# Moving four pieces of VectorE work in the first steps of a fused attention and two-layer kernel

## The chip, the cores and the metric

The kernel runs on one core of a Trainium2 chip. Times are device microseconds of one execution. TensorE (PE in the rows) multiplies matrices, VectorE (DVE), ScalarE (ACT) and GpSimd (POOL) work on elements, SyncE (SP) issues the DMAs. Each engine runs its own instructions in the order in which the program writes them and waits for other engines by semaphores.

## The reference

```python
# q, k, v: 4 batches, 8 heads, 576 positions, 64 wide
scores = scale * q @ k.T
ret = scores * Dmat              # gamma ** (i - j) where i >= j, else 0
x = (ret @ v), heads side by side   # 2304 tokens x 512
h = x @ w_in                     # 512 -> 2048, weights arrive as float64
g = h * sigmoid(1.702 * h)
x = g @ w_out                    # 2048 -> 512
h = x @ w2_in                    # 512 -> 1024
solu = h * softmax(h)
ln = (solu - mean) / sqrt(var + 1e-6) * g_ln
out = ln @ w2_out                # 1024 -> 512
```

## The kernel before

**Stages.** First comes the attention, in eight pairs of (batch, head pair) units, `k` from 0 to 7. Then the first layer runs in 24 steps. A step `s` is a generation `g` (a quarter of the 2048 hidden features), a pair `p` of token tiles (2 x 384 tokens) and a half `i` of the generation's features. Steps 0 to 5 are generation 0: steps 0 and 1 are the first pair of token tiles, 2 and 3 the second, 4 and 5 the third. The second layer follows at the end.

**A step's products.** `emit_h` does not multiply a 2 x 2 block of tiles with eight products but with seven, by sums of x and of the weights (Strassen's scheme in a form with few additions). It uses four PSUM banks, A, C, B and D. TensorE (line 705) makes, in this order, A, C, B, then A and C again on top, then D, then B again on top. VectorE adds the intermediate results (line 711): c12 from B before B gets its second product, then C, then c21, D and B. ScalarE then applies the gate (lines 682 and 684), and the low part of the result is a subtraction (line 685), on VectorE in steps 1 and 3 and mostly on GpSimd elsewhere. `emit_y` (line 779) multiplies the gated features with `w_out`. In steps 1 and 3 it ends with the second token tile, whose four results go to the banks that the step's own h leaves.

**Two parts of each number.** Matrices are held as a high and a low part, so that each product is three products of TensorE. ScalarE writes the high part by a cast (line 660 for x, line 292 for weights), GpSimd the low part by a subtraction (lines 662 and 293).

**Work beside the products.** Three kinds of VectorE work are put between the steps:

- *Conversions* (`convert`, lines 277 to 279): float64 weights, loaded by DMA into one of two raw buffers, become float32 in three instructions, by way of a PSUM bank named `conv`. Once one is done, the next load into the same buffer is issued (line 263).
- *Combinations* (`queue_combine`, line 284, 128x256): four differences of converted weights, t1 to t4, of which t2 and t4 need the ones before. ScalarE's casts of the weights (line 292) follow.
- *Sums of x* (`combine_x`, lines 653 and 284, 128x768): s1, s2, s3 and s4 of the next pair of token tiles, from which x's parts are split.

Conversions and combinations stand in one queue, `bg`. `slot(n)` takes work of cost n from its front at the place in the program where it is called: a conversion costs 3, a combination 0.5. The table `PACE` gives n for the first steps, one number inside `emit_h` after the last additions and one at the step's end. Casts of weights that a combination feeds are held for a later `slot`, three at a time.

Of the kernel before, what the change touches and what calls it, by code (L numbers as in the profile page):

```python
# [39 lines left out]
PAIRS = [[p if g % 2 == 0 else NPR - 1 - p for p in range(NPR)] for g in range(GENS)]  # L40
# [108 lines left out]

WARM = 7  # L150
LATE = 3
PACE = ((2, 6), (0, 6), (5, 0), (0, 6), (6, 0), (5, 0))


class Build:
# [195 lines left out]
    def pace(self, s, part):  # L351


        if s < len(PACE):
            return PACE[s][part]
        most = lambda t, b: ((6, 0), (6, 0), (6, 0), (6, 0), (6, 3), (6, 3))[t % 6][b]
# [651 lines left out]
    def run(self):  # L1008
# [8 lines left out]
        def spin(n):  # L1017
            for _ in range(n):
                nc.tensor.matmul(wb[:, 0:P], warm, warm, start=True, stop=True)
# [4 lines left out]
        def load_w():  # L1024
            dst, piece = self.first_loads.pop(0)
            self.load_raw(dst, self.source(piece))
# [13 lines left out]
        sums, split_x = self.combine_x(0)  # L1040

        def make_x(*js):
            for j in js:
                split_x(j)
                self.xready += 1
# [3 lines left out]
        for k in range(NPAIR):  # L1049
            u = 2 * k  # L1050
            nxt = k + 1 < NPAIR
            if k + 2 < NPAIR:
                self.decay_q(u + 4, u + 5)
            if k == 0:
                pt, o = self.bank("T0"), []
                self.scores(0)
                spin(2)
                self.scale_v(0)
                self.states(0, pt)
                o.append(self.bank("o0"))  # L1060
                self.within(0, o[0], True)
                self.scores(1)
                ends = [self.bank("e0")]
                self.last_scores(0, ends[0])
                self.last_masks(0, ends[0])
                spin(4)
                self.scale_v(1)
                self.states(1, pt)
                self.scan(0, pt)
                o.append(self.bank("o1"))  # L1070
                self.within(1, o[1], True)
                pt = self.bank("T1")
                self.scale_v(2)
                self.states(2, pt)
                ends.append(self.ybank("e1"))
                self.across(0, o, ends, False)
                self.scale_v(3)
                self.states(3, pt)
                for i in range(2):
                    self.take(i, o[i], False)  # L1080
                for i in range(2):
                    self.take(i, ends[i], True)
                self.scan(1, pt)
                self.scores(2)
                self.last_scores(1, ends[0])
                self.last_masks(1, ends[0])
                self.scores(3)
            else:
                if nxt:
                    self.scale_v(u + 2)  # L1090
                if k > 1:
                    self.scores(u)
                    self.scores(u + 1)
                o, ends = [self.bank(f"o{u}")], [self.bank(f"e{k}")]
                o.append(self.bank(f"o{u + 1}"))
                for i in ((), (), (), (), (0,), (1,), (3,), (2,))[k]:
                    sums[i]()
                self.slot((0, 0, 0, 0, 0.5, 0.5, 0, 6)[k])
                ends.append(self.ybank(f"e{u + 1}"))
                self.across(k, o, ends, True)  # L1100
                if nxt:
                    pt = self.bank(f"T{k + 1}")
                    self.states(u + 2, pt)
                for i in range(2):
                    self.take(u + i, ends[i], True)
                if not nxt:
                    steps = self.emit_h(0)
                    next(steps)
                for i in range(2):
                    self.within(u + i, o[i], False)  # L1110
                if nxt:
                    self.scale_v(u + 3)
                    self.states(u + 3, pt)
                    self.last_scores(k + 1, ends[0])
                    make_x(*((), (), (), (), (1,), (2,), (4,))[k])
                    self.slot((0, 3, 3, 1, 0, 0, 0)[k])
                    self.scan(k + 1, pt)
                    self.last_masks(k + 1, ends[0])
                for i in range(2):
                    self.take(u + i, o[i], False)  # L1120
            if k == 0:
                for i, part in ((NU, 0), (NU, 1), (NU + 1, 1)):
                    self.load_unit(i, part)
                load_w()
                self.load_unit(NU + 1, 0)
            for i in (u + NU, u + 1 + NU):
                if k and i < 2 * NPAIR:
                    for part in range(2):
                        self.load_unit(i, part)
            for _ in range((0, 0, 0, 0, 1, 1, 2, 2)[k]):  # L1130
                load_w()
            make_x(*((), (0,), (3,), (5,), (), (), (), (6,))[k])
# [3 lines left out]
        for g, p, i in STEPS:  # L1136
            s = 6 * g + 2 * PAIRS[g].index(p) + i
            at = PAIRS[g].index(p)
            if s == 0:
                self.queue_rest()  # L1140
            self.last = g == GENS - 1
            after = PAIRS[g][at + 1] if at + 1 < NPR else None
            self.quiet = 0 < g < GENS - 1 and i == 0 and after is not None
            for j in self.emit_h(s) if s else chain([0], steps):
                while s == 0 and self.first_loads:
                    load_w()
                if s == 0:
                    self.store_x(p, j)
                if s + 1 == NSTEP and j == 1:
                    self.flush()  # L1150
                if s == 1 and j == 1:
                    self.slot(0)
                if s == 1 and j == 2:
                    sums[3]()
                if s == 2 and j == 4:
                    sums, split = self.combine_x(PAIRS[0][2])
                    for fn in sums:
                        fn()
                if i and after is not None:
                    if g == 0:  # L1160
                        if s != 1 or j != 6:
                            split(j)
                            self.store_x(after, j)
                    else:
                        self.load_x(after, j)
            if s == 1:
                sums[2]()
                split(6)
                self.store_x(after, 6)
            if s == 0:  # L1170
                sums, split = self.combine_x(PAIRS[0][1])
                for fn in sums[:2]:
                    fn()
            if s + 1 == NSTEP:
                self.open_second()
                for k, u in ((2, (1, 1)), (3, (2, 0)), (4, (2, 1))):
                    self.fetch(u, self.wo[k].rearrange("r (a b) -> r a b", a=2))
                self.nys = 0
                ys, y1, y2 = (self.split_y(p) for p in range(3))
                for fn in ys:  # L1180
                    fn()
            f = list(range(FG * g, FG * g + FG))
            y = lambda t, a, n, *r, **k: self.emit_y(g, p, t, f[a:a + n], *r, **k)
            if s == 0:
                y(0, 0, 2, True, False)
                y(1, 0, 2, bank=self.bank)
            elif s == 1:
                y(0, 2, 2, False)
                y(1, 2, 2, add=True, bank=self.bank)
            elif g == 0 and not i:  # L1190
                y(0, 0, 2, True, False)
            elif g == 0:
                y(0, 2, 2, False)
                if after is not None:
                    y(1, 0, FG, bank=self.bank)
            elif i:
                y(0, 0, FG)
            else:
                pg, pp, _ = STEPS[s - 1]
                self.emit_y(pg, pp, 1, range(FG * pg, FG * pg + FG))  # L1200
            self.done.add(("y", s))
            self.ring = self.bank if g == 0 and i == 0 else self.ybank
            self.quiet = g > 0 and i == 0 and at + 1 < NPR
            if s not in (2, 4):
                self.slot(self.pace(s, 1))
            self.quiet, self.ring = False, self.bank
        for fn in y1[:6] + y2[:4]:
            fn()
# [126 lines left out]
```

## Time and profile before

| | |
|---|---|
| median of 3 runs | 648.93 us (648.71 to 649.03) |
| profiled execution | 648.17 us, of which the span of the trace is 646.4 us |
| TensorE, VectorE, ScalarE, GpSimd busy | 638.0 (99%), 448.9 (69%), 283.9 (44%), 304.5 (47%) us |
| HBM, mean over the span | 187 GB/s |

The busy shares are means over the whole span. The stage that the change touches lies between about 34 and 125 us, and a row there says more than the share. In a row of the timeline the first number is the start in us from the span's start and the second the time from the start of the first to the end of the last of the instructions that the row holds. What stands in brackets at the end is the time in which the engine was idle ahead of it, and what ended that.

### The profile page before, as it was taken

The page shows a single profiled execution, that of the slowest core. Times are in us where ns is not written, and L with a number is a line of the kernel's source. Part 1 is how long each engine was busy: PE and PEld are TensorE (multiplying, and loading weights), DVE is VectorE, ACT ScalarE, POOL GpSimd, SP SyncE. Part 2 cuts the span into 40 slices and gives each one's busy share as a digit, 9 for nine tenths or more (in the row PEclk, how much of TensorE's full clock was granted, in tenths as well). Part 3 has the DMA queues.
Part 4 walks back from the last instruction along what each step waited for, and adds up shares of the span by engine and source line. Part 5 has one row for each costly group of instructions (what it writes and reads, how often), then busy time and mean ns, then how long its engine had stood idle before and what let it go on. Part 6 is the DMA issues. An engine that isn't in the chain of part 4 may idle for free.

```text
span 646.4 us, 11295 instructions
## 1 busy us (share of the span) xinstructions
PE 638.0 (99%) x4316; PEld 597.9 (93%) x4316; DVE 448.9 (69%) x746; ACT 283.9 (44%) x614; POOL 304.5 (47%) x312
## 2 busy tenths in 40 slices
PE   8999999999999999999999999999999999999998
PEld 7989989999999999999999999998888888888887
DVE  2998979746477587567576454455998977787770
ACT  3566564746434343334343424343444552454231
POOL 3498595955335574336574424352324430442100
PEclk9999999999999999999999999999999999999999
DMA  8999466662575835756644959489100000000001
GB/s 330 411 416 419 179 230 242 239 234 97 188 318 203 334 131 163 275 229 256 260 149 137 361 219 337 165 301 359 48 18 32 34 17 16 34 17 16 33 32 50
DMA packets 30006, 121.78 MB, mean 188 GB/s; under 512 B 3328, under 2 KB 3840, under 8 KB 29952
## 3 DMA queue, kind: packets, MB, share of 16 engines
q1 hardware_dynamic: 29808, 120.99, 49.5%
q8 instruction: 34, 0.56, 0.3%
q14 instruction: 20, 0.16, 0.1%
q10 hardware_dynamic: 144, 0.07, 0.0%
HBM read 88.28 MB, written 32.77 MB: 187 GB/s over the span
## 4 chain that ended last, share of the span: by engine, by line
PE 83%; DVE 2%; issue 0%; ACT 0%; DVEq 0%
PE y L779 28%; PE o L933 15%; PE h L843 13%; PE h_B L705 7%; PE h_A L705 7%; PE h_C L705 7%; PE h_D L705 3%; PE zT L907 2%; DVE mem L284 1%; DVE mem L711 0%; DVE mem L653 0%; DVE conv L278 0%; DVE mem L279 0%; DVE conv L277 0%; DVE g L685 0%
## 5 line engine op out<-in xcount | busy, mean ns | idle before, releaser
L685 POOL TENSOR_TENSOR g<-mem,g 128x384 fp32r<-128x384 f32 x84 | 87.7, 1055 | 143.1 <-ACT mem L684 140.0
L293 POOL TENSOR_TENSOR win<-mem,win 128x256 fp32r<-128x256 f32 (+2 forms) x59 | 53.8, 941 | 56.7 <-ACT win L292 52.6
L779 PE MATMUL y<-g,wo 128*128 128x384 f32 x432 | 77.9, 334 | 0.0
L779 PEld LDWEIGHTS y<-g,wo 128*128 128x128 f32 x432 | 75.0, 188 | 0.3 <-DVE mem L788 0.2
L711 DVE TENSOR_TENSOR mem<-h_B,mem 128x384 f32<-128x384 f32 x48 | 26.6, 555 | 65.1 <-PE h_B L705 65.0
L788 DVE TENSOR_TENSOR mem<-y,mem 128x384 f32<-128x384 f32 x76 | 38.2, 550 | 26.6 <-PE y L779 26.4
L284 DVE TENSOR_TENSOR mem<-mem 128x256 f32<-128x256 f32 (+2 forms) x49 | 47.8, 1005 | 0.7
L662 POOL TENSOR_TENSOR x<-mem,x 128x384 fp32r<-128x384 f32 x42 | 43.4, 1065 | 5.6 <-ACT x L660 5.6
L843 PE MATMUL h<-ut,win 128*128 128x512 f32 x168 | 42.9, 390 | 0.0
L894 POOL TENSOR_TENSOR mem<-mem 128x1 f32<-128x1 f32 x18 | 10.3, 573 | 68.7 <-DVE mem L893 62.5
L293 POOL TENSOR_TENSOR ws<-mem,ws 128x512 fp32r<-128x512 f32 (+1 forms) x32 | 36.5, 1159 | 10.9 <-ACT ws L292 10.8
L933 PE MATMUL o<-u,zs 128*128 128x512 f32 (+1 forms) x171 | 41.7, 388 | 0.0
L719 ACT COPY mem<-h_A 128x384 f32<-128x384 f32 x24 | 11.6, 485 | 67.9 <-PE h_A L705 66.9
L779 PE MATMUL y<-g,wo0dt.float32r 128*128 128x384 f32 x216 | 40.8, 335 | 0.1
L779 PE MATMUL y<-g,wo1dt.float32r 128*128 128x384 f32 x216 | 40.3, 334 | 0.0
L849 DVE TENSOR_TENSOR mem<-h,mem 128x512 f32<-128x512 f32 x36 | 24.6, 687 | 22.4 <-PE h L843 12.5
L933 PE MATMUL o<-wo,zs 128*128 128x512 f32 (+1 forms) x171 | 40.0, 378 | 0.0
L779 PEld LDWEIGHTS y<-g,wo0dt.float32r 128*128 128x128 f32 x216 | 37.6, 188 | 0.6 <-DVE mem L279 0.4
L779 PEld LDWEIGHTS y<-g,wo1dt.float32r 128*128 128x128 f32 x216 | 37.7, 188 | 0.0
L843 PEld LDWEIGHTS h<-ut,win 128*128 128x128 f32 x168 | 31.4, 188 | 6.4
L933 PEld LDWEIGHTS o<-wo,zs 128*128 128x128 f32 x171 | 31.0, 188 | 6.0
L933 PEld LDWEIGHTS o<-u,zs 128*128 128x128 f32 x171 | 29.9, 189 | 5.1
(154 smaller groups left out, 1506.1 us busy)
## 6 DMA issues: line engine op xcount, KB each, us to landing
x<-xd SPq DMA_DIRECT2D x42, 768.0 KB, 8.6
xd<-x SPq DMA_DIRECT2D x21, 768.0 KB, 4.7
mem<-in_w SPq DMA_DIRECT2D x28, 512.0 KB, 5.5
in<-in_att SPq DMA_DIRECT2D x16, 576.0 KB, 9.9
in<-in_att SPq DMA_DIRECT2D x16, 544.0 KB, 9.2
out<-mem SPq DMA_DIRECT2D x17, 256.0 KB, 2.0
mem<-in_w2in SPq DMA_DIRECT2D x8, 512.0 KB, 4.0
wdt<-ws SPq DMA_DIRECT2D x8, 512.0 KB, 5.4
```

Of the source, the lines that this page charges most:

```text
L284: self.nc.vector.tensor_tensor(o, a, b, ALU.subtract)
L293: self.nc.gpsimd.tensor_tensor(lo, src, f32(hi), ALU.subtract)
L662: (engine or self.nc.gpsimd).tensor_tensor(x[:, 1, k], a[:, k], f32(x[:, 0, k]), ALU.subtract)
L685: engine.tensor_tensor(gs[:, 1], u, f32(gs[:, 0]), ALU.subtract)
L705: nc.tensor.matmul(o, w[:, c:c + P], x[j][:, m, k], start=(start and i == 0), stop=(stop and i == 5), skip_group_check=True,)
L711: add = lambda o, a, b: nc.vector.tensor_tensor(o, a, b, ALU.add)
L779: nc.tensor.matmul(o[m], w[:, c:c + P], gs[:, b], start=(begin and i == 0), stop=(end and i == 2),)
L788: nc.vector.tensor_tensor(y[:, m], o[m], y[:, m], ALU.add)
L843: nc.tensor.matmul(o, a[:, l, k], w[:, m], start=(start and i == 0), stop=(stop and i == 5), skip_group_check=True,)
L849: add = lambda o, a, b: nc.vector.tensor_tensor(o, a, b, ALU.add)
L907: nc.tensor.transpose(pt[:, b * P:(b + 1) * P], u[:, w:w + P], ident)
L933: nc.tensor.matmul(o[:, 0:n], z[:, a, k], w[:, b, p * n:(p + 1) * n], start=(k == 0 and i == 0), stop=(k == FB - 1 and i == 2),)
```

## The change

It moves four pieces of work to other places in the program. No instruction is added or removed on an engine that computes.

- One combination goes from the fifth pair of the attention (`k` = 4) to the end of the fourth (`k` = 3).
- The last two conversions of step 0 go ahead of the first two sums of x for the second pair.
- The four sums of x for the third pair go from the middle of step 2's h to its end. The four combinations of step 2 stay behind them.
- One conversion goes from the end of step 2's h into step 3's h, after D's product.

```diff
-PACE = ((2, 6), (0, 6), (5, 0), (0, 6), (6, 0), (5, 0))
+PACE = ((2, 6), (0, 6), (0, 0), (0, 6), (6, 0), (5, 0))
...
-                self.slot((0, 0, 0, 0, 0.5, 0.5, 0, 6)[k])
+                self.slot((0, 0, 0, 0, 0, 0.5, 0, 6)[k])
...
-                    self.slot((0, 3, 3, 1, 0, 0, 0)[k])
+                    self.slot((0, 3, 3, 1.5, 0, 0, 0)[k])
...
-                if s == 2 and j == 4:
-                    sums, split = self.combine_x(PAIRS[0][2])
-                    for fn in sums:
-                        fn()
+                if s == 3 and j == 5:
+                    self.slot(3)
...
-            if s == 0:
-                sums, split = self.combine_x(PAIRS[0][1])
-                for fn in sums[:2]:
+            if s == 2:
+                sums, split = self.combine_x(PAIRS[0][2])
+                for fn in sums:
                     fn()
+                self.slot(2)
...
             if s not in (2, 4):
                 self.slot(self.pace(s, 1))
+            if s == 0:
+                sums, split = self.combine_x(PAIRS[0][1])
+                for fn in sums[:2]:
+                    fn()
```

On VectorE, between step 0's combinations and step 1's c12 (the two 768-wide rows are the sums of x):

```order
 L284 TENSOR_TENSOR mem<-mem 128x256 x4
+L277 TENSOR_SCALAR conv<-mem 128x512
+L278 SCALAR_TENSOR_TENSOR conv<-mem,conv 128x512
+L279 SCALAR_TENSOR_TENSOR mem<-mem,conv 128x512
+L277 TENSOR_SCALAR conv<-mem 128x512
+L278 SCALAR_TENSOR_TENSOR conv<-mem,conv 128x512
+L279 SCALAR_TENSOR_TENSOR mem<-mem,conv 128x512
 L653 TENSOR_TENSOR mem<-mem 128x768
 L284 TENSOR_TENSOR mem<-mem 128x768
```

The same two conversions stood right behind these two sums before, so conversions and sums have changed places.

On VectorE in step 2, from c12 on (the three rows that move are c21, D and B; the 768-wide ones are the third pair's sums):

```order
 L711 TENSOR_TENSOR mem<-h_B,mem 128x384
 L711 TENSOR_TENSOR h_C<-h_C,mem 128x384
+L711 TENSOR_TENSOR mem<-h_B,mem 128x384
+L711 TENSOR_TENSOR h_D<-h_D,mem 128x384
+L711 TENSOR_TENSOR h_B<-mem 128x384
 L653 TENSOR_TENSOR mem<-mem 128x768
 L284 TENSOR_TENSOR mem<-mem 128x768
 L284 TENSOR_TENSOR mem<-mem 128x2x384
 L284 TENSOR_TENSOR mem<-mem 128x768
-L711 TENSOR_TENSOR mem<-h_B,mem 128x384
-L711 TENSOR_TENSOR h_D<-h_D,mem 128x384
-L711 TENSOR_TENSOR h_B<-mem 128x384
```

The additions c21, D and B now stand ahead of the four sums.

On VectorE behind that, from step 2's combinations into step 3's h (g_1101 and g_1102 are the first two gates of step 3; the first line 711 row is its c12):

```order
 L284 TENSOR_TENSOR mem<-mem 128x256 x4
-L277 TENSOR_SCALAR conv<-mem 128x512
-L278 SCALAR_TENSOR_TENSOR conv<-mem,conv 128x512
-L279 SCALAR_TENSOR_TENSOR mem<-mem,conv 128x512
 L711 TENSOR_TENSOR mem<-h_B,mem 128x384
 L685 TENSOR_TENSOR g_1101<-h_A,g_1101 128x384
 L711 TENSOR_TENSOR h_C<-h_C,mem 128x384
 L685 TENSOR_TENSOR g_1102<-h_C,g_1102 128x384
+L277 TENSOR_SCALAR conv<-mem 128x512
+L278 SCALAR_TENSOR_TENSOR conv<-mem,conv 128x512
+L279 SCALAR_TENSOR_TENSOR mem<-mem,conv 128x512
```

The conversion has gone from ahead of c12 to behind the second gate's subtraction; c21, D and B of step 3 follow it. With it, the load that refills its raw buffer goes on SyncE's queue from ahead of the third pair's stores of x to behind the fifth of these seven.

## Rows read from the trace of the kernel before

**Rows 1.** Busy time in a window: length, then each engine's busy us; granted clock.

```profile
125.00:600.00 475.00, 475.00 (x2584) 448.78 (x2583) 323.05 (x548) 198.24 (x429) 212.71 (x212) 1.00 0.46 171
```

**Rows 2.** Timeline, TensorE's weight loads with idle time ahead, 81 to 124 us.

```profile
81.25 0.99 PEld L705 LDWEIGHTS h_A<-x,win1dt.float32r 128*128 128x128 f32 x6 [0.71 <-ACT mem L786]
...
84.10 1.01 PEld L705 LDWEIGHTS h_B<-x,win1dt.float32r 128*128 128x128 f32 x6 [0.79 <-DVE mem L279]
...
95.03 0.99 PEld L779 LDWEIGHTS y<-g,wo2dt.float32r 128*128 128x128 f32 x6 [0.49 <-DVE g L685]
...
111.20 1.00 PEld L705 LDWEIGHTS h_C<-x,win1dt.float32r 128*128 128x128 f32 x6 [0.62 <-ACT mem L684]
...
115.92 1.00 PEld L705 LDWEIGHTS h_D<-x,win1dt.float32r 128*128 128x128 f32 x6 [0.60 <-DVE mem L279]
...
123.34 1.00 PEld L779 LDWEIGHTS y<-g,wo0dt.float32r 128*128 128x128 f32 x6 [0.18 <-DVE g L685]
```

**Rows 3.** Timeline of VectorE's SBUF additions and GpSimd's gates in narrow windows.

```profile
75.13 0.42 DVE L284 TENSOR_TENSOR mem<-mem 128x256 f32<-128x256 f32 x1
...
75.93 1.24 DVE L284 TENSOR_TENSOR mem<-mem 128x256 f32<-128x256 f32 x1
...
105.66 0.96 DVE L284 TENSOR_TENSOR mem<-mem 128x768 f32<-128x768 f32 x1
105.68 1.81 POOL L685 TENSOR_TENSOR g<-mem,g 128x384 fp32r<-128x384 f32 x1 [1.10 <-ACT mem L684]
...
106.53 1.77 DVE L284 TENSOR_TENSOR mem<-mem 128x768 f32<-128x768 f32 x1
```

**Rows 4.** Timeline of VectorE, the scan behind pair 3 of the attention.

```profile
38.17 1.22 DVE L547 TENSOR_TENSOR_SCAN st<-mem,T 128x512 f32<-128x512 f32 x1 [1.18 <-PE T L538]
```

**Rows 5.** Timeline from the end of step 0 to step 1's gate.

```profile
79.68 0.86 ACT L786 COPY mem<-y 128x384 f32<-128x384 f32 x2
...
81.85 0.68 DVE L277 TENSOR_SCALAR conv<-mem 128x512 uint32<-128x512 uint32 x1
...
83.90 2.00 POOL L662 TENSOR_TENSOR x<-mem,x 128x384 fp32r<-128x384 f32 x2 [0.82 <-ACT x L660]
...
85.86 1.30 POOL L293 TENSOR_TENSOR wo2dt.float32r<-mem,wo2dt.float32r 128x512 fp32r<-128x512 f32 x1
...
89.10 0.56 DVE L685 TENSOR_TENSOR g<-h_A,g 128x384 fp32r<-128x384 f32 x1 [1.13 <-ACT h_A L684]
```

**Rows 6.** Timeline of TensorE: step 2's last product, step 3's first.

```profile
104.50 1.20 PE L705 MATMUL h_B<-x,win0dt.float32r 128*128 128x384 f32 x6
...
109.70 1.20 PE L705 MATMUL h_A<-x,win1dt.float32r 128*128 128x384 f32 x6
```

**Rows 7.** Timeline of VectorE and ScalarE in step 3.

```profile
113.73 0.68 DVE L277 TENSOR_SCALAR conv<-mem 128x512 uint32<-128x512 uint32 x1
...
115.51 0.66 ACT L292 CAST win<-mem 128x512 fp32r<-128x512 f32 x1
...
115.79 0.55 DVE L711 TENSOR_TENSOR mem<-h_B,mem 128x384 f32<-128x384 f32 x1
...
118.95 0.56 DVE L685 TENSOR_TENSOR g<-h_C,g 128x384 fp32r<-128x384 f32 x1 [1.68 <-ACT h_C L684]
...
120.01 0.57 DVE L711 TENSOR_TENSOR h_D<-h_D,mem 128x384 f32<-128x384 f32 x1
...
120.98 0.54 ACT L682 ACTIVATE g<-h_D 128x384 fp32r<-128x384 f32 x1
...
122.73 0.56 DVE L685 TENSOR_TENSOR g<-h_B,g 128x384 fp32r<-128x384 f32 x1 [0.23 <-ACT h_B L684]
```

**Rows 8.** Timeline and DMA issues: stores of x, loads of weights (KB, us to landing), step 4's c12.

```profile
126.18 2.27 SPq L668 DMA_DIRECT2D xd<-x  x2
...
mem<-in_w SPq DMA_DIRECT2D x6, 512.0 KB, 5.5
...
134.15 0.56 DVE L711 TENSOR_TENSOR mem<-h_B,mem 128x384 f32<-128x384 f32 x1 [6.23 <-PE h_B L705]
```

## The prediction

> **What bounds the kernel now.** I read the busy time by windows first. Between 125 and 600 us TensorE is busy for all 475.00 us, at a granted clock of 1.00 [rows 1]. So whatever TensorE loses or wins before 125 us arrives unchanged at the end, and the change acts only before that. Next I read TensorE's gaps as idle time of its weight loads. Between 80 and 125 us there are six [rows 2]: step 1's h_A (0.71, ScalarE's copy of y), h_B (0.79, VectorE's conversion), step 1's y (0.49, VectorE's gate), step 3's h_C (0.62, ScalarE's gate of step 2), h_D (0.60, a conversion) and step 3's y (0.18, VectorE's gate). Last I followed VectorE, ScalarE and GpSimd there by the timeline, because the engine that TensorE waits for at 95.03 and 123.34 is the one that decides.
>
> **A view that sets the prices.** VectorE's additions whose inputs both lie in SBUF have two durations [rows 3]. A combination of 256 columns takes 0.42 us when GpSimd is idle and 1.24 when GpSimd works. A sum of 768 columns takes 0.96 or 1.77. The second one was issued at 106.53, GpSimd's gate ended at 105.68 + 1.81 = 107.49, and the sum ended at 108.30: it waited for GpSimd's whole instruction and then ran 0.81. GpSimd in turn needed 1.81 instead of about 1.0, having been issued together with the sum before. So they take turns, one whole instruction each. VectorE's additions that read PSUM stay at 0.55, and a conversion's instruction at 0.68 while GpSimd splits x [rows 7]. The Trainium skill says this as a rule (SBUF — State Buffer, Who interferes with whom): a VectorE instruction with two SBUF inputs and a GpSimd instruction that reads SBUF exclude each other, and the second waits until the first is done. By that rule, with which the trace agrees, the moved sums cost what the turns below say; with the lone durations of 0.95 and 0.45 for every sum and combination the step-2 chain below would end 5.0 us sooner, and the total would be that of rival 1.
>
> **A combination one pair sooner.** The third combination moves from pair 4 to the end of pair 3. There VectorE idles 1.18 us for TensorE's T [rows 4]; a combination of 0.42 to 1.24 us fits into that, or nearly. The place it leaves also stood ahead of a scan that waits for TensorE. I take 0; if the cover is short by one GpSimd turn, 0.3, which TensorE's queue of small matmuls hides.
>
> **Step 0's conversions ahead of x's sums.** Bounds on the gain: h_B's 0.79, no more. The conversions need y's banks back, and ScalarE's first copy starts at 79.68, so they start at about 80.15 instead of 81.85 [rows 5]. Two of them at 2.06 (113.73 to 115.79 [rows 7]) end at 84.3, early enough for h_B: the 0.79 goes. But the two sums now follow, and GpSimd makes x0's differences from 83.90 (1.0 each), then wo2's (1.30) [rows 5]. By turns: first sum 84.9 to 85.7, x0's second half to 86.7, second sum to 87.5, wo2 to 88.8, then s4's sum to 89.6; c12 (0.55, a PSUM operand) lies between. Step 1's first gate subtraction, at 89.10 before behind ScalarE [rows 5], starts at about 89.7: +0.6. ScalarE is behind too, since its cast of the second sum now waits for 87.5. Everything up to the y wait at 95.03 follows this chain, so h_B's 0.79 is only waited out there. Term: **+0.6**. From below: if VectorE wins the turns, ScalarE's gate is the later one and the term is -0.6; from above, one more turn, +1.0 (these are estimates from the rows named).
>
> **Third pair's sums behind step 2's own.** Now c21, D and B of step 2 stand ahead of four sums. They can start when TensorE ends h_B, 104.50 + 1.20 = 105.7 [rows 6] and no longer behind the sums. That frees step 2's banks early: h_C's 0.62 goes. Three at 0.55 end at 107.35. Then, in turns with GpSimd's two gates of step 2 (of the shape of x's differences, so 1.0 each), 0.95 for a sum that waits for nothing, 0.8 for one behind GpSimd and 0.3 for a combination behind it: first sum to 108.3, gate D 109.3, second sum 110.1, gate B 111.1, third sum 111.9. Step 3's first difference of x comes 2.65 after h_A starts (81.25 to 83.90 [rows 2, 5]), so at 109.70 + 2.65 = 112.35 [rows 6]; the fourth sum is in before it and ends at 112.8. But the four combinations, which before ended by 113.73, now meet it: x0's first half to 113.8, t1 114.1, second half 115.1, t2 115.4, x1 116.4, t3 116.7, x1 117.7, t4 **118.0**. That is 4.3 late. What waits for t4: on VectorE c12 of step 3 and all behind it; on ScalarE the second of three weight casts, which stood at 115.51 + 0.65 = 116.15 [rows 7] and now stands at 118.0, with g_C's gate right behind. VectorE's subtraction of g_C goes from 118.95 to 120.8: **+1.85**. TensorE's last h_B of step 3, which waits for c12, stalls too, but that wait lies inside the same lateness. From below: if the combinations get ahead of x0 (they miss it by 0.45 us), ScalarE is even 0.6 earlier, h_C's stall being gone. From above: if the fourth sum also falls behind x0, 1.0 more.
>
> **One conversion inside step 3's h.** It leaves its place ahead of c12, so h_D's 0.60 goes. It now stands behind g_C's subtraction and ahead of c21, D and B. VectorE waits for ScalarE before g_C (1.68 idle [rows 7]), but the conversion is behind that wait, not in it. So c21 and D come 2.06 later. ScalarE took D's gate only 0.4 after D was ready (120.01 + 0.57 against 120.98 [rows 7]), which covers 0.4. The last gate subtraction, at 122.73 before, moves by 1.85 + 2.06 - 0.4 = **+3.5**, and TensorE's y of step 3 waits for exactly that one [rows 2]. Also queued behind the conversion: y's second bank is the conversion's, free at about 123.4, ahead of the third and fourth.
>
> **Its DMA.** The conversion's reload of weights is now issued behind five stores of x; the fourth and fifth leave from 126.18 on, the fifth at about 128. With 5.5 to landing it is there at 133.6, its conversion ends at 135.7, and step 4's c12, at 134.15 with 6.23 of VectorE idle ahead [rows 8], would be 1.5 late on the old time base. TensorE is itself over 3 us later by then. I take 0, at most 1.5.
>
> **Sum.** 0 + 0.6 + 3.5 + 0 = +4.1. The profiled execution took 648.17 (span 646.4 and 1.8 around it); it becomes 652.3. The median of the runs is 648.93, 0.76 above the profiled one; I forecast on it: **653.0 us**. Bounds: below -0.6 (step 1) with -0.6 + 2.06 - 0.4 (step 3) = +0.5; above 1.0 + 4.5 = +5.5.
>
> **Rivals.**
> 1. *Only the conversion's place costs.* GpSimd doesn't come between the combinations, t4 ends by about 114.6, and step 3 loses 2.06 - 0.4 - 0.6 = 1.1; with step 1 at 0 to 0.6, +1.1 to +1.7: about 650.2. For it: the miss of 0.45 is small. Against: four combinations one by one need four lucky turns. Between it and the forecast lies one or two turns fewer, 651 to 652.
> 2. *It is faster.* The three waits of 0.79, 0.62 and 0.60 go and nothing takes their place: -2.0, 646.9. The deciding point: the last gate subtraction of step 3 must not come later than 122.73, so combinations and conversion would both have to lie in VectorE's idle time. For it: VectorE has 1.68 idle there. Against: the conversion is queued behind that idle time, and c21 behind the conversion.
> 3. *Worse still.* The fourth sum misses its turn as well and the reload holds up step 4: +5.5 to +6, 654.7.
>
> **How the numbers follow.** Forecast, +3 to +4.7: 0.48. One or two turns fewer, +1.7 to +3: 0.18. Rival 1, +0.5 to +1.7: 0.14. Rival 2: 0.12. Rival 3: 0.08. A measurement here tells about 0.2%, 1.3 us. Rival 1 splits near that bound, so: faster 0.11, same 0.13, slower 0.76. The range 649.9 to 654.4 leaves out rival 2, a little of rival 1 and most of rival 3.
>
> **What would show it.** In the profile of the changed kernel: h_B, h_C and h_D of steps 1 and 3 without their waits; the combinations of step 2 at about 1.3 each, the last ending some 4 us after 113.73; ScalarE idle between step 3's weight casts; a new wait of step 3's second h_B for VectorE; and a wait of about 2 us or more in step 3's y for VectorE's gates. The prediction is wrong if the combinations run ahead of x0's differences, or if step 3's y does not wait for VectorE.

## The result, and the profile after

The changed kernel takes **653.48 us** (median of 6 runs, 652.27 to 653.94) beside 649.06 for the kernel before on the same chip (6 runs, 648.71 to 650.26): ratio 1.0061, 95% interval 1.0048 to 1.0074. It is slower by more than 0.2%. A second set of 6 runs, on another occasion, gave 652.30 beside 648.87, ratio 1.0048 (1.0030 to 1.0066). The profiled execution took 653.72, span 651.9, which is 5.5 more than before.

TensorE's weight loads with idle time ahead, from 81 to 128 us of the changed kernel, answer to [rows 2]:

```profile
81.96 0.99 PEld L705 LDWEIGHTS h_A<-x,win1dt.float32r 128*128 128x128 f32 x6 [0.71 <-ACT mem L786]
88.66 0.99 PEld L705 LDWEIGHTS h_B<-x,win1dt.float32r 128*128 128x128 f32 x6 [0.48 <-DVE mem L711]
...
96.17 0.99 PEld L779 LDWEIGHTS y<-g,wo2dt.float32r 128*128 128x128 f32 x6 [0.71 <-DVE g L685]
118.75 1.01 PEld L705 LDWEIGHTS h_B<-x,win1dt.float32r 128*128 128x128 f32 x6 [1.83 <-DVE mem L711]
126.38 0.30 PEld L779 LDWEIGHTS y<-g,wo0dt.float32r 128*128 128x128 f32 x2 [1.77 <-DVE g L685]
127.32 1.36 PEld L779 LDWEIGHTS y<-g,wo0dt.float32r 128*128 128x128 f32 x6 [0.65 <-DVE g L685]
```

The waits of h_B for a conversion (0.79), of h_C (0.62) and of h_D (0.60) are gone. In their place stand two waits for c12 (0.48 in step 1, 1.83 in step 3) and a longer wait for the gates of step 3 (1.77 and 0.65 where 0.18 stood).

VectorE and ScalarE in step 3 answer to [rows 7]; the last three rows are the conversion's reload of weights and, from step 4, a conversion and c12, beside [rows 8]:

```profile
115.99 0.61 ACT L292 CAST win<-mem 128x512 fp32r<-128x512 f32 x1
118.26 1.36 ACT L292 CAST win<-mem 128x768 fp32r<-128x768 f32 x2 [1.66 <-DVE mem L284]
...
118.15 0.55 DVE L711 TENSOR_TENSOR mem<-h_B,mem 128x384 f32<-128x384 f32 x1
...
121.15 0.56 DVE L685 TENSOR_TENSOR g<-h_C,g 128x384 fp32r<-128x384 f32 x1 [1.52 <-ACT h_C L684]
121.62 0.68 DVE L277 TENSOR_SCALAR conv<-mem 128x512 uint32<-128x512 uint32 x1
...
124.26 0.57 DVE L711 TENSOR_TENSOR h_D<-h_D,mem 128x384 f32<-128x384 f32 x1
124.73 1.03 DVE L711 TENSOR_TENSOR h_B<-mem 128x384 f32<-128x384 f32 x1
...
126.71 0.56 DVE L685 TENSOR_TENSOR g<-h_B,g 128x384 fp32r<-128x384 f32 x1 [0.39 <-ACT h_B L684]
...
129.00 0.41 SPq L263 DMA_DIRECT2D mem<-in_w  x1
...
134.94 0.70 DVE L277 TENSOR_SCALAR conv<-mem 128x512 uint32<-128x512 uint32 x1 [5.18 <-DMA mem<-in_w]
...
139.68 0.56 DVE L711 TENSOR_TENSOR mem<-h_B,mem 128x384 f32<-128x384 f32 x1 [2.52 <-PE h_B L705]
```

ScalarE is idle for 1.66 us between two weight casts until the last combination is done, at 118.2. Gate C's subtraction follows at 121.15, then the conversion, then D, B, and the last gate subtraction at 126.71. Step 4's c12 waits 2.52 for TensorE, so the reload comes early enough. The chain that ended last runs through the same places (start, us, what):

```profile
112.66 2.12 DVE mem L284 x2
...
114.80 1.20 DVE mem L284 x2
...
117.01 1.22 DVE mem L284
...
118.26 1.36 ACT win L292 x2
...
121.62 0.69 DVE conv L277
...
127.32 9.13 PE y L779 x42
```

The last of these rows holds something that no step of the prediction has: 42 products of y took 9.13 us, where 42 of 0.173 (12 take 2.08 in this step in the trace of e3 below) are 7.3. The windows there (columns as in [rows 1]) say why:

```profile
127.00:128.00 1.00, 0.68 (x3) 0.68 (x4) 0.65 (x2) 1.00 (x4) 1.00 (x2) 0.92 0.61 258
128.00:129.00 1.00, 1.00 (x5) 1.00 (x5) 0.97 (x2) 0.73 (x2) 1.00 (x2) 0.50 1.02 430
129.00:130.00 1.00, 1.00 (x5) 1.00 (x5) 0.73 (x2) 0.00 (x0) 1.00 (x2) 0.50 0.92 375
130.00:131.00 1.00, 1.00 (x5) 1.00 (x4) 0.00 (x0) 0.00 (x0) 1.00 (x2) 0.50 1.10 369
131.00:132.00 1.00, 1.00 (x7) 1.00 (x6) 0.00 (x0) 0.00 (x0) 1.00 (x2) 0.87 0.98 215
```

From 128 to 131 us the granted clock is 0.50, TensorE's lower level (1.2 GHz), behind the waits at 118.75, 126.38 and 127.32.

**All traces in one table.** The times are taken from the rows of each trace: the start of ScalarE's first copy of y behind step 0 (79.68 in [rows 5]), and, counted from that start, step 1's last gate subtraction, gate C's subtraction in step 3, and step 3's last gate subtraction; then the time from there to the end of the span.

```
kernel                     copy   step 1  gate C  last of step 3   rest    span
before                    79.68   14.74   39.27   43.05          523.67   646.4
changed                   80.39   15.17   40.76   46.32          525.19   651.9
changed, second trace     80.53   15.17   40.77   46.34          523.63   650.5
e7 combination alone      80.96   14.77   39.31   43.08          523.66   647.7
e1 step 0's part alone    80.51   15.14   39.68   43.45          523.64   647.6
e2 sums put back          80.06   15.17   39.72   45.97          524.67   650.7
e3 conversion late        80.11   15.17   40.74   44.51          525.68   650.3
e4 late differences       81.57   15.16   38.99   45.11          523.62   650.3
e6 before, conv. late     81.84   14.76   39.29   43.06          529.00   653.9
e8 before, conv. sooner   80.39   14.77   40.03   44.31          523.60   648.3
```

Between the copy and step 3's last subtraction two traces of one kernel agree within 0.02 us, so these columns show single tenths. The change costs 0.43 in step 1, 1.49 - 0.43 = 1.06 more by gate C, and (46.32 - 40.76) - (43.05 - 39.27) = 1.78 between gate C and the last: 3.27 in all. The rest of the difference of the spans, 5.5 - 3.27, is 0.71 ahead of the first copy and 1.52 behind step 3, the stretch at the lower clock.

### The profile page after: what moved, and what is told of

Same layout as the page of the kernel before. It is cut to its first block, busy times and chain, and to the rows that moved or that the text cites. A ratio compares the mean times of both kernels' runs of the same rounds, so it can differ in the third digit from the quotient of the medians.

```text
span 651.9 us, 11295 instructions
## 1 busy us (share of the span) xinstructions
PE 639.9 (98%) x4316; PEld 599.1 (92%) x4316; DVE 451.0 (69%) x746; ACT 284.4 (44%) x614; POOL 305.6 (47%) x312
## 4 chain that ended last, share of the span: by engine, by line
PE 82%; DVE 2%; issue 1%; ACT 1%; ACTq 0%; DVEq 0%
PE y L779 27%; PE o L933 15%; PE h L843 13%; PE h_B L705 7%; PE h_C L705 7%; PE h_A L705 7%; PE h_D L705 3%; PE zT L907 2%; DVE mem L284 1%; DVE h_B L711 0%; ACT win L292 0%; DVE g L685 0%; DVE h_D L711 0%; DVE mem L711 0%; ACT g L682 0%
## 5 line engine op out<-in xcount | busy, mean ns | idle before, releaser
L662 POOL TENSOR_TENSOR x<-mem,x 128x384 fp32r<-128x384 f32 x42 | 44.9, 1102 | 8.6 <-ACT x L660 8.6
L277 DVE TENSOR_SCALAR conv<-mem 128x512 uint32<-128x512 uint32 x44 | 30.2, 686 | 7.7 <-DMA mem<-in_w 5.5
```

Of the source, the lines that this page charges most:

```text
L277: nc.vector.tensor_scalar(x, high, 3, 0x3FFFFFF8, ALU.logical_shift_left, ALU.bitwise_and)
L662: (engine or self.nc.gpsimd).tensor_tensor(x[:, 1, k], a[:, k], f32(x[:, 0, k]), ALU.subtract)
```

## The experiments

Each was timed against the kernel before on the same chip; that kernel's median was 648.87 on both occasions.

**e7, the combination alone** (the kernel before with this edit):

```diff
-                self.slot((0, 0, 0, 0, 0.5, 0.5, 0, 6)[k])
+                self.slot((0, 0, 0, 0, 0, 0.5, 0, 6)[k])
...
-                    self.slot((0, 3, 3, 1, 0, 0, 0)[k])
+                    self.slot((0, 3, 3, 1.5, 0, 0, 0)[k])
```

> The kernel before with one part of the change alone: one combination of weights a pair sooner. Theory: it fills an idle stretch of VectorE, TensorE waits for it nowhere, 648.7 to 649.2 beside 648.9. Rival: TensorE's idle time at 61 us that ends with nothing the profile shows (0.19 us before, 1.0 in the changed kernel) belongs to this part: 649.6 to 649.9.

Measured: 648.99, ratio 0.9997 (0.9986 to 1.0008). The theory holds: this part costs nothing. Its columns in the table are those of before within 0.04, but for the first, and the span that holds it.

**e1, step 0's part alone** (the kernel before with this edit):

```diff
-            if s == 0:
-                sums, split = self.combine_x(PAIRS[0][1])
-                for fn in sums[:2]:
-                    fn()
...
             if s not in (2, 4):
                 self.slot(self.pace(s, 1))
+            if s == 0:
+                sums, split = self.combine_x(PAIRS[0][1])
+                for fn in sums[:2]:
+                    fn()
```

> The kernel before with one part of the change alone: step 0's last conversions stand in front of the first two sums of x. Theory: TensorE's wait of 0.79 us for h_B in step 1 goes, but VectorE and ScalarE do the same work and step 1's last gates come no sooner, so TensorE waits it out at step 1's y instead; the sums that now meet GpSimd's copies cost 0.2 to 0.6 us. Time 649.2 to 649.7 beside 649.1 before. Rival: the 0.79 us is won, 648.3. If the wait of 1.02 us at 61 us in the changed kernel (0.19 before) is of this part, it shows here too, and the time is 0.7 higher than either says.

Measured: 649.41, ratio 1.0007 (0.9998 to 1.0015), and 0.40 more at step 1's last subtraction. The theory holds and the gain of 0.79 does not come. The wait at 61 us is here too (0.97), but the time is not 0.7 higher for it. In the changed kernel one sees where it goes (ScalarE and VectorE in step 1):

```profile
86.48 0.84 ACT L660 CAST x<-mem 128x768 fp32r<-128x768 f32 x1 [0.52 <-DVE mem L653]
88.22 0.83 ACT L660 CAST x<-mem 128x768 fp32r<-128x768 f32 x1 [0.90 <-DVE mem L284]
...
88.53 1.57 DVE L284 TENSOR_TENSOR mem<-mem 128x768 f32<-128x768 f32 x1
90.03 0.54 DVE L685 TENSOR_TENSOR g<-h_A,g 128x384 fp32r<-128x384 f32 x1
...
93.51 1.10 DVE L711 TENSOR_TENSOR h_B<-mem 128x384 f32<-128x384 f32 x1
```

ScalarE's casts now wait for the sums, and a sum beside GpSimd's work takes 1.57 and is not done when ScalarE's part of gate A is (89.83). Counted from the copy, gate A's subtraction is 0.22 late by that (9.64 against 9.42). The rest of the 0.43 comes later in the step, with B's addition, which takes 1.10 here and 0.84 before.

**The changed kernel once more**, unaltered.

> The changed kernel unaltered, for a second trace of it and more times. If the 0.7 us by which it stood later before its first moved row (TensorE's wait of 1.02 us at 61 us) and the clock at half speed from 128 to 131 us belong to the order of its rows, both show again and the time is 653 to 654; if the first is chance and the second comes in some executions alone, the times fall into two groups, near 652.3 with a mean clock of 1.000 and near 653.7 with 0.997.

Measured: 652.30 (651.91 to 654.01). The second trace has the first wait again (1.29 us at 61 us) but not the low clock: from 128 to 130 us it is at 1.00, and the column "rest" is that of before.

```profile
128.00:130.00 2.00, 2.00 (x13) 2.00 (x12) 1.86 (x3) 0.88 (x3) 2.00 (x3) 1.00 0.95 396
```

Of the 12 runs of the changed kernel, 7 have a mean granted clock of 1.000 and a median of 652.29; 5 have 0.997 and a median of 653.81. The 1.52 between them is as large as the 1.52 of the table. So the second half of the expectation holds: the low clock comes in some executions alone. That it stands behind step 3 in all five is not shown, since only one of them was traced, and a mean of 0.997 does not tell where the clock was low: the traces of e4 and e8, also at 0.997, have it in the first 20 us instead.

The wait at 61 us stands ahead of every moved row but the combination. e7, with the combination, has 0.21 there and yet reaches the first copy later (80.96) than any of the kernels with the long wait; e1, whose rows up to there are those of before, has 0.97. So no moved row ahead of it makes this wait. It is long in five of the six traces that have step 0's part and in none of the four that have not; why, and what ends it, the traces do not show. I read the first column as scatter between executions.

**e2, the sums put back** (the changed kernel with this edit; the conversion stays in step 3):

```diff
-PACE = ((2, 6), (0, 6), (0, 0), (0, 6), (6, 0), (5, 0))
+PACE = ((2, 6), (0, 6), (2, 0), (0, 6), (6, 0), (5, 0))
...
+                if s == 2 and j == 4:
+                    sums, split = self.combine_x(PAIRS[0][2])
+                    for fn in sums:
+                        fn()
...
-            if s == 2:
-                sums, split = self.combine_x(PAIRS[0][2])
-                for fn in sums:
-                    fn()
-                self.slot(2)
```

> The changed kernel with the third pair's sums of x and the combinations put back to where they stood before (sums inside step 2's h, combinations at its end); the conversion stays inside step 3's h. Theory: the last combination ends at about 114 to 115 us instead of 118.2, so the subtraction of step 3's gate C is back at about 119 to 119.7, and of the change's 4.4 us only the conversion in the gate chain (2.06 less at most 0.4) and step 1's few tenths are left: 651.0 to 651.5, and up to 1.5 more if the clock falls near 128 us as in the changed kernel. Rival one: the conversion costs nothing and the sums' place all of it: 649.3 to 649.7. Rival two: the sums' place costs nothing and the conversion all: 653.5, as the changed kernel.

Measured: 653.02, ratio 1.0065 (1.0051 to 1.0079). The first half held: gate C is back (39.72, which is 0.45 over before, 0.43 of it step 1's). The time did not: from gate C to the last subtraction it takes 6.25, more than the changed kernel's 5.56. VectorE in step 3:

```profile
119.78 0.56 DVE L685 TENSOR_TENSOR g<-h_C,g 128x384 fp32r<-128x384 f32 x1 [2.26 <-ACT h_C L684]
...
123.37 1.72 DVE L711 TENSOR_TENSOR h_B<-mem 128x384 f32<-128x384 f32 x1
125.01 0.54 DVE L685 TENSOR_TENSOR g<-h_D,g 128x384 fp32r<-128x384 f32 x1
```

The last addition, B, has both inputs in SBUF. It takes 0.56 alone (the last row of the groups shown under e4), 1.03 in the changed kernel and 1.72 here, where it falls on one of GpSimd's splits of weights. So the conversion's price is not 2.06 less a cover; it also moves B into another turn. By the time alone rival two came nearest: with the conversion in place, putting the sums back wins only 46.32 - 45.97 = 0.35 at step 3's end, and runs of like mean clock differ by the same 0.36 (651.93 against 652.29 at 1.000; at the lower clocks a median of 653.45 against 653.81).

**e3, the conversion behind step 3's gates** (the changed kernel with this edit):

```diff
-                if s == 3 and j == 5:
-                    self.slot(3)
...
+            if s == 3:
+                self.slot(3)
             if s not in (2, 4):
                 self.slot(self.pace(s, 1))
```

> The changed kernel with step 3's conversion taken out of h and put behind step 3's last gate; the sums stay behind step 2's own. Theory: additions C2+C1 and D no longer stand behind 2.06 us of conversion, ScalarE is the next limit 0.4 to 0.5 later, so step 3's y starts 1.5 to 1.7 us sooner: 651.8 to 652.0 beside 653.5 of the changed kernel; and 1.2 to 1.5 less again, 650.4 to 650.7, if the fall of the clock near 128 us goes with the shorter waits. VectorE has some 6 us idle in step 4, so the conversion costs nothing there. Rival: the conversion was covered by ScalarE's casts, and the time is the changed kernel's, 653.5.

Measured: 654.25 (652.07 to 655.13), ratio 1.0079 (1.0063 to 1.0096): no gain at all. Yet the theory's own step is there: from gate C to the last subtraction it takes 3.77, as before (3.78), and y waits only 0.18. The gain is given back in step 4 (TensorE, SyncE, VectorE):

```profile
125.24 1.31 PE L779 MATMUL y<-g,wo0dt.float32r 128*128 128x384 f32 x6 [0.18 <-DVE g L685]
...
140.76 1.31 PE L705 MATMUL h_B<-x,win0dt.float32r 128*128 128x384 f32 x6 [1.72 <-DVE mem L711]
...
132.62 1.37 SPq L263 DMA_DIRECT2D mem<-in_w  x2
...
138.02 0.69 DVE L277 TENSOR_SCALAR conv<-mem 128x512 uint32<-128x512 uint32 x1 [8.73 <-DMA mem<-in_w]
```

The load that reuses the conversion's buffer now goes out at 132.62, behind the last store of x, instead of 129.00. The next conversion starts at 138.02, ahead of c12 in VectorE's queue, and TensorE waits 1.72 for c12.

**e6, the same edit on the kernel before** (its conversion at step 2's end taken behind step 3's gates), to test that reading:

```diff
-PACE = ((2, 6), (0, 6), (5, 0), (0, 6), (6, 0), (5, 0))
+PACE = ((2, 6), (0, 6), (2, 0), (0, 6), (6, 0), (5, 0))
...
+            if s == 3:
+                self.slot(3)
             if s not in (2, 4):
                 self.slot(self.pace(s, 1))
```

> The kernel before with one edit: the conversion at step 2's end stands behind step 3's last gate instead. Theory (from the experiment that did the same to the changed kernel): ScalarE sets step 3's gates, so step 3's y starts as before, within 0.3 us; but the weight load that waits for this conversion goes out behind all seven stores of x, near 132 us instead of 116, lands near 138, and step 4's first addition on VectorE comes at about 140: TensorE, which is 1.5 to 1.9 us earlier here than in that experiment, waits 3 to 3.6 us for it. Time 651.5 to 652.7 beside 648.9. Rival: the load has slack, and taking 2.06 us out from in front of step 3's first addition ends TensorE's wait of 0.60 us for h_D: 648.3 to 648.9.

Measured: 655.68 (653.90 to 658.32), ratio 1.0096 (1.0073 to 1.0119). Step 3 ends as before (43.06 against 43.05), so without the 0.60 for h_D nothing is won; and the wait in step 4 is the one foretold. TensorE, SyncE and VectorE:

```profile
142.88 1.92 PE L705 MATMUL h_B<-x,win0dt.float32r 128*128 128x384 f32 x6 [3.57 <-DVE mem L711]
...
134.57 1.38 SPq L263 DMA_DIRECT2D mem<-in_w  x2
...
140.13 0.69 DVE L277 TENSOR_SCALAR conv<-mem 128x512 uint32<-128x512 uint32 x1 [10.57 <-DMA mem<-in_w]
```

The time is 3 us over the expectation. In the trace the clock is low at two places: the mean of the first 20 us is 0.91, and behind the wait the window from 144 to 146 us has the lower level.

```profile
0.00:20.00 20.00, 16.56 (x208) 14.56 (x210) 5.71 (x11) 6.81 (x16) 7.91 (x21) 0.91 0.90 343
...
144.00:146.00 2.00, 2.00 (x8) 2.00 (x7) 1.14 (x3) 0.40 (x2) 1.01 (x1) 0.50 0.55 195
```

The first copy comes 2.16 later than before (81.84 against 79.68), and behind step 3 it takes 529.00 - 523.67 = 5.33 more, of which the wait is 3.57; about 1.8 is left for the second place.

**e4, two of GpSimd's differences later** (the changed kernel; in step 3 the splits of x's parts 0 and 1 are queued behind part 2's):

```diff
-                    if g == 0:
+                    if s == 3 and j < 3:
+                        split(j, low=j == 2)
+                        if j == 2:
+                            for n in range(2):
+                                split(n, high=False)
+                            for n in range(3):
+                                self.store_x(after, n)
+                    elif g == 0:
```

Here `split` makes ScalarE's casts where `high` is true and GpSimd's differences where `low` is.

> The changed kernel with GpSimd's differences of the parts 0 and 1 of the third pair's x queued behind that of part 2, so that GpSimd has less work while the combinations run. Theory of turns (two additions with SBUF operands and GpSimd's instructions alternate, each whole): each combination met one difference in the changed kernel and took 1.13 to 1.24 us instead of 0.8; here at most one is met, the last ends at 115.5 to 116.4 instead of 118.2, and step 3's y starts 1.8 to 2.4 us sooner: 651.0 to 651.7 beside 653.5. Rival (the combinations are long for another reason, such as the order on VectorE alone): they still take 1.1 to 1.2 us each, and the time is 653.5.

Measured: 650.92 (12 runs), ratio 1.0031 (1.0020 to 1.0043): 1.4 to 2.6 less than the changed kernel's two medians. Groups of instructions on VectorE by shape, of the changed kernel from 108.4 to 118.1 us and then of e4 from 109.5 to 116.2 (count, busy us, mean ns; line 712 of e4 is line 711 of the others):

```profile
L284 DVE TENSOR_TENSOR mem<-mem 128x256 f32<-128x256 f32 x4 | 4.7, 1203 | 0.0
L284 DVE TENSOR_TENSOR mem<-mem 128x768 f32<-128x768 f32 x3 | 4.1, 1432 | 0.1
```

```profile
L284 DVE TENSOR_TENSOR mem<-mem 128x768 f32<-128x768 f32 x3 | 4.1, 1432 | 0.1
L284 DVE TENSOR_TENSOR mem<-mem 128x256 f32<-128x256 f32 x4 | 1.5, 418 | 0.0
...
L712 DVE TENSOR_TENSOR h_B<-mem 128x384 f32<-128x384 f32 x1 | 0.6, 556 | 0.0
```

This is the plainest evidence for turns. VectorE's queue is the same. Of the engines that compute only GpSimd's order is changed, which in e4 begins its differences at 116.39, and the combinations fall from 1203 to 418 ns in the mean, while the sums, beside the same gates of GpSimd, stay at 1432. The stores of x go out later too (from 120.35 on instead of 115.68), but they are not the reason: in the changed kernel the combinations at 113.53 and 114.80 start ahead of the first store and take 1.24 and 1.13. By the Trainium skill (SBUF — State Buffer, Who interferes with whom), a VectorE instruction with two SBUF inputs contends with a GpSimd instruction that reads SBUF, and the lock between them is exclusive. These numbers agree. The gain at the last subtraction is 46.32 - 45.11 = 1.21, not 1.8 to 2.4: gate C comes 1.77 sooner, but B's addition falls on another of GpSimd's splits (1.59 instead of 1.03). The 7 runs of e4 at a mean clock of 1.000 have a median of 649.97, 2.3 under the changed kernel's 652.29; where the 1.1 beyond these 1.21 comes from is not shown.

**e8, the conversion two instructions sooner** (the kernel before; the conversion inside step 3's h, ahead of gate C's addition instead of behind its subtraction):

```diff
-PACE = ((2, 6), (0, 6), (5, 0), (0, 6), (6, 0), (5, 0))
+PACE = ((2, 6), (0, 6), (2, 0), (0, 6), (6, 0), (5, 0))
...
+                if s == 3 and j == 3:
+                    self.slot(3)
```

> The kernel before with one edit: the conversion at step 2's end stands inside step 3's h, as in the change, but two VectorE instructions sooner, between gate A's subtraction and gate C's addition, where VectorE then waits 1.7 to 2.3 us for ScalarE. Theory (the price of a conversion is its place in the gate chain): it lies in that wait, gate C's addition ends near 118.2 us, 0.2 us behind ScalarE's own time for it, and step 3's last subtraction comes 0 to 0.4 us later than before: 648.9 to 649.4; the weight load goes out behind three stores, early enough. Rival (a conversion anywhere in step 3's h costs its 1.8 to 2.4 us, as it did behind gate C): 650.7 to 651.3.

Measured: 650.25 (12 runs, one of 659.75 and the others from 649.23 to 651.25), ratio 1.0015 (1.0003 to 1.0027), between theory and rival. VectorE in step 3, and GpSimd's splits of weights beside B's addition:

```profile
118.92 0.56 DVE L711 TENSOR_TENSOR h_C<-h_C,mem 128x384 f32<-128x384 f32 x1
120.42 0.56 DVE L685 TENSOR_TENSOR g<-h_C,g 128x384 fp32r<-128x384 f32 x1 [0.94 <-ACT h_C L684]
...
121.95 1.81 DVE L711 TENSOR_TENSOR h_B<-mem 128x384 f32<-128x384 f32 x1
...
121.50 3.40 POOL L293 TENSOR_TENSOR win<-mem,win 128x768 fp32r<-128x768 f32 x2
```

Half of the theory holds: gate C moves by 0.76, not by 2. The idle time before gate C was not all cover, since ScalarE waits for this very addition (0.64 us in this trace). And B's addition takes 1.81 where it took 0.76 before, so the last subtraction is 1.26 late. A conversion's place matters, but of the two places tried inside step 3's h neither is free.

None of these versions beats the kernel before; e7 equals it.

## Why the prediction was right, and where its sizes were off

- **A combination sooner: 0.** Shown by e7.
- **Step 1: +0.6.** Measured 0.43 (0.40 alone in e1), and h_B's 0.79 came back as other waits, as the step said. The term is 0.2 too large. At its own place, gate A, only 0.22 came; the rest is B's addition, which the step did not have. Its reason for h_B is not the right one, though the wait went: B's first product needs only the first of the two conversions (done at 83.36 + 0.69 = 84.05 before, 82.44 + 0.69 = 83.13 in the changed kernel), not the second, which ends at 84.3 by the step's own sum, later than h_B started before.
- **Sums behind step 2's own: +1.85 at gate C.** The mechanism is shown: by-shape durations in e4, ScalarE idle between its casts, and gate C back at its time in e2 once the sums are back in their place. The size is 1.49 - 0.43 = 1.06, so the term is 0.8 too large. The step gave each turn of a difference and a combination 1.3 us; three turns took 118.23 - 114.80 = 3.43, or 1.14 each. It also had the last combination end at 118.0; with the later first copy (0.71) and step 1 (0.43) taken off it ended at about 117.1.
- **One conversion in step 3's h: 2.06 - 0.4.** Measured 1.78 against 1.66; e3, without it, has 3.77 there as before. What the step did not see is that the price changes with what GpSimd does when B's addition comes: 6.25 - 3.78 = 2.47 in e2, 2.34 in e4.
- **Its DMA: 0.** Right for this kernel: in both its traces step 4's c12 still waits for TensorE (2.52 and 1.18). The reason given, that TensorE is late itself, is not enough, as e3 and e6 show: with the load behind the last two stores TensorE waits 1.72 and 3.57. With the load ahead of two stores it is 0.
- **The sum: +4.1.** The rows show 3.27 up to step 3's end, and the 7 runs at a mean clock of 1.000 are 652.29 - 648.87 = 3.4 over the kernel before. The other 5 runs, at 0.997, are 1.5 longer; in the one of them that was traced, the lower clock behind step 3 is that 1.5. So the first 6 runs' median is near the forecast of 653.0 partly by luck: a cost that the prediction left out, 1.5 in some executions, makes up for 0.8 by which its terms were too large.
- **The rivals.** Rival 1 (only the conversion's place costs) fell with the changed kernel's rows and e4: GpSimd does come between the combinations. But the terms do not add up as the sum has them. At step 3's last subtraction, over the 43.45 of e1, the sums' place alone costs 1.06 (e3, 44.51), the conversion's place alone 2.52 (e2, 45.97), and both together 2.87 (46.32), not 3.58. B's addition meets other work of GpSimd each time: it takes 1.72 in e2 and 1.03 in the changed kernel, which is 0.69 of the 0.71 between. Rival 2 (faster) fell with the result, and e1, e3 and e6 show why: each wait that went was waited out at the next product that needed the gates. Rival 3's late reload did not occur here, but it is real, as e3 and e6 show.

That the lower clock follows from TensorE's waits is not shown. It stands behind idle times between TensorE's products of 1.45 us in the first trace of the changed kernel, 2.54 in e2 (at 0.50 from 126 to 128 us) and 3.57 in e6. It is absent behind 1.44 in the second trace, 1.72 in e3 and 1.95 in e4.

## What to carry to other kernels

A wait of the engine that bounds the kernel is worth something only if the chain behind it also gets shorter: here three waits of 0.6 to 0.8 us went, and the gates at the end of the step decided the time all the same. Before VectorE work with two SBUF inputs is moved, look at what GpSimd does at the new place, since each such instruction may wait for a whole one of GpSimd's, and a piece that moves can push a later one beside other work. And a moved conversion takes its DMA along: what counts is where the next load then stands in the queue, behind which stores.

## What was not expected of the hardware

- The same addition of 128x384, both inputs in SBUF, took 0.56, 0.76, 1.03, 1.59, 1.72 and 1.81 us, by what GpSimd was doing.
- TensorE's granted clock was 0.50 (1.2 GHz) for about 3 us behind its waits in the changed kernel, in one of its two traces. 5 of its 12 executions have a mean clock of 0.997 and are 1.5 us longer; the kernel before had a mean clock of 0.997 or less in 3 of 46 executions timed beside the experiments.
- In three traces (e4, e6, e8) the clock was at 0.91 in the first 20 us, where the kernel before has 1.00, and the first copy came at 80.39 to 81.84 us instead of 79.68; without that, it came at up to 80.96 (e7).
